# First batch's q norms partly from squares instead of a block product, and the late outputs stored in two halves

**Chip, cores, metric.** One core of one Trainium2 chip. The time is device microseconds of one execution; the profile's span, from the first to the last instruction, is about 1.8 us shorter. Times in the text are us from the start of the span unless they are called execution times.

## The reference, cut to what matters

```python
# B, N, C = 4, 6144, 256;  tau = 1
qn = q / (norm(q, axis=1) + 1e-6);  kn = k / (norm(k, axis=1) + 1e-6)   # over N
s = kn.transpose(0, 2, 1) @ qn / tau            # per batch a 256 x 256 matrix
a = softmax(s, -1);  x = v @ a                  # 24576 x 256
h = max(x @ w1, x @ w2, x @ w3);  out = h @ w_out        # d_ff = 768
```

Only the 256 x 256 softmax of the **first** batch stands alone at the head of the kernel. Those of the others are computed beside the big products.

## The kernel before

The kernel folds `a` into the weights (`aw = a @ w`), so the bulk is `h = v @ aw` (line L360) and `out = h @ w_out` (L380). For batch 0 it loads k and q, takes the q-by-k product into two PSUM banks (`gram`), and the q-by-q product of each half beside it in the same bank; its diagonal holds the squared norms.

```python
        for tp in range(NG // 2):                       # 24 pairs of rows
            for j in range(CC):
                PE.matmul(ps[j][:, 0:C], lhsT=qt[:, tsl, jsl], rhs=kt[:, tsl, :], ...)          # L178
                PE.matmul(ps[j][:, C:C + P], lhsT=qt[:, tsl, jsl], rhs=qt[:, tsl, jsl], ...)    # L180
    # ... cut ...
    def softmax_t(ps, rkb):
        for j in range(CC):                             # masked sum = diagonal        # L253
            DVE.tensor_tensor_reduce(out=scr, in0=ps[j][:, C:C + P], in1=ident, ..., accum_out=n2q[:, j:j + 1])
        ACT.activation(out=lnq, in_=n2q, func=AF.Ln)
        ACT.activation(out=rq, in_=lnq, func=AF.Exp, scale=-0.5, bias=neg_ln_tau)
        return exp_t([ps[j][:, 0:C] for j in range(CC)], rkb, rq)
    # ... cut ...
    ps = gram(0)
    for i in range(6):                                  # fill TensorE's time           # L436
        PE.matmul(warm_ps, lhsT=ident, rhs=warm, ...)
    et = softmax_t(*ps)
    v_transpose_pe(0)
    rinv = aw_first(et, aw)                             # first products with et        # L306
    v_transpose(1)                                      # transposing transfer of v of chunk 1, on SyncE's queue
    hold_loads(1)                                       # GpSimd reads the transposed tile: waits until it has landed
    POOL.dma_start(out=wo_sb, in_=moe_w_out...)         # only then the load of w_out   # L450
    # ... cut ...
            if t == TPC - 1:
                SP.dma_start(out=out_r[gi // NCH, gi % NCH], in_=st["o"])               # L386
```

## Time and profile before

| | before |
|---|---|
| execution time, three runs | 575.91 to 576.07 us |
| TensorE busy | 555.2 of 574.1 us, 97% |
| warm-up weight loads start | 34.00 |
| first h product (L360) | 37.47 |
| first o product (L380), asks for w_out | 50.58 |
| last store issued, end of span | 570.72, 574.09 |

The first is in the timeline near 50 us (columns: start, duration, engine, line, operation):

```profile
45.05 0.19 POOL L447 COPY guard<-vt_sb 128x1 bf16<-128x1 bf16 x1 [7.99 <-DMA vt_sb<-v_sb]
45.28 0.83 POOL L450 DMA_DIRECT2D wo_sb<-in_moe_w_out_dram  x1
...
50.58 0.82 PE L380 MATMUL o_ps<-wo_sb,ht_sb 128*128 128x256 bf16 x6
```

The load of w_out is issued only when the transposed v of chunk 1 has landed. It takes 5.2 us from issue to landing (the profile's time to landing of this tile), so it is there at 50.5, and TensorE asks for it at 50.58. There is 0.1 us to spare.

The second is at the very end, in the waits of SyncE's queue (engine and line, what it waited for, us in total, times, longest):

```profile
SPq L533 <- DMA out_dram<-o_sb: 1.6, 3, 0.9
```

The program ends when SyncE has gone through a row of waits for its stores, and three of these waits find a store that is still under way.

### The profile page before, as it was taken

The page shows a single profiled execution, that of the slowest core. Times are in us where ns is not written, and L with a number is a line of the kernel's source. Part 1 is how long each engine was busy: PE and PEld are TensorE (multiplying, and loading weights), DVE is VectorE, ACT ScalarE, POOL GpSimd, SP SyncE. Part 2 cuts the span into 40 slices and gives each one's busy share as a digit, 9 for nine tenths or more (in the row PEclk, how much of TensorE's full clock was granted, in tenths as well). Part 3 has the DMA queues.
Part 4 walks back from the last instruction along what each step waited for, and adds up shares of the span by engine and source line. Part 5 has one row for each costly group of instructions (what it writes and reads, how often), then busy time and mean ns, then how long its engine had stood idle before and what let it go on. Part 6 is the DMA issues. An engine that isn't in the chain of part 4 may idle for free.

```text
span 574.1 us, 9430 instructions
## 1 busy us (share of the span) xinstructions
PE 555.2 (97%) x3361; PEld 331.9 (58%) x3362; DVE 407.6 (71%) x639; ACT 308.6 (54%) x537; POOL 227.3 (40%) x235
## 2 busy tenths in 40 slices
PE   3789999999999999999999999999999999999997
PEld 3665555555755555555575555555575555555565
DVE  0058777777577778777748777777848778778775
ACT  1044567677454466776735447767646444444443
POOL 4232357876721028776761007777760000000000
PEclk9999999999999999999999999999999999999999
DMA  9999998995598128887378526888535234322111
GB/s 143 107 145 153 137 181 124 156 136 122 89 124 160 56 79 149 129 157 121 75 130 134 117 69 102 157 133 136 121 83 124 66 83 129 74 92 75 56 73 75
DMA packets 76095, 65.63 MB, mean 114 GB/s; under 512 B 52368, under 2 KB 62224, under 8 KB 76048
## 3 DMA queue, kind: packets, MB, share of 16 engines
q0 software_dynamic: 18928, 26.48, 39.1%
q1 hardware_dynamic: 56976, 38.41, 23.5%
q8 instruction: 26, 0.43, 0.3%
q14 instruction: 21, 0.17, 0.1%
q10 hardware_dynamic: 144, 0.13, 0.1%
HBM read 78.64 MB, written 25.17 MB: 181 GB/s over the span
## 4 chain that ended last, share of the span: by engine, by line
PE 94%; DMA 5%; issue 0%; DVE 0%; POOL 0%; POOLq 0%
PE h_ps L360 65%; PE o_ps L380 21%; DMA q_sb<-in_q_dram 3%; PE gram L235 3%; PE ew_ps L282 2%; DMA k_sb<-in_k_dram 2%; PE o_ps L401 0%; PE gram L178 0%; PE ew_ps L306 0%; PE n_ps L216 0%; PE warm_ps L436 0%; PE n_ps L218 0%; PE gram L180 0%; POOL k_sb L99 0%; PE vt_ps L343 0%
## 5 line engine op out<-in xcount | busy, mean ns | idle before, releaser
L360 PE MATMUL h_ps<-vt_sb,aw_sb 128*128 128x512 bf16 (+1 forms) x1764 | 407.2, 375 | 0.1
L365 DVE TENSOR_TENSOR s_mx<-h_ps,s_mx 128x512 bf16<-128x512 f32 (+1 forms) x294 | 198.8, 676 | 97.6 <-ACT s_mx L364 96.5
L360 PEld LDWEIGHTS <-aw_sb 128*128 128x128 bf16 x1764 | 171.8, 98 | 161.0 <-DVE aw_sb L288 2.8
L364 ACT ACTIVATE s_mx<-h_ps 128x512 bf16<-128x512 f32 (+1 forms) x294 | 172.3, 586 | 131.4 <-PE h_ps L360 130.0
L366 DVE TENSOR_TENSOR ht_sb<-h_ps,s_mx 128x512 bf16<-128x512 f32 (+1 forms) x294 | 200.2, 681 | 31.4 <-PE o_ps L380 0.5
L204 POOL TENSOR_TENSOR acc<-acc,sq 128x768 f32<-128x768 f32 x90 | 147.6, 1650 | 70.7 <-ACT sq L198 70.5
L380 PE MATMUL o_ps<-wo_sb,ht_sb 128*128 128x256 bf16 x1128 | 153.9, 273 | 0.0
L380 PEld LDWEIGHTS <-ht_sb 128*128 128x128 bf16 x1128 | 110.4, 98 | 52.0
L383 ACT ACTIVATE o_sb<-o_ps 128x512 f32<-128x512 f32 x94 | 56.1, 597 | 82.6 <-PE o_ps L380 82.6
L110 POOL DMA_DIRECT2D v_sb<-in_v_dram x48 | 26.8, 562 | 89.0 <-DMA vt_sb<-v_sb 87.1
L198 ACT ACTIVATE sq<-q_sb 128x768 bf16<-128x768 fp8e4 x48 | 40.5, 845 | 0.0
L198 ACT ACTIVATE sq<-k_sb 128x768 bf16<-128x768 fp8e4 x48 | 40.1, 835 | 0.0
L201 POOL CAST acc<-sq 128x768 f32<-128x768 bf16 x6 | 4.9, 821 | 63.1 <-ACT sq L198 63.1
L102 POOL DMA_DIRECT2D q_sb<-in_q_dram x32 | 17.7, 552 | 10.7 <-DMA k_sb<-in_k_dram 9.7
L166 PE MATMUL kk<-k_sb 128*128 128x256 fp8e4 x48 | 7.8, 339 | 11.6 <-DVE k_sb L152 5.4
L235 PE MATMUL gram<-k_sb,q_sb 128*128 128x512 fp8e4 x144 | 16.8, 277 | 0.0
L99 POOL DMA_DIRECT2D k_sb<-in_k_dram x29 | 15.9, 551 | 1.0 <-POOLq L519 0.8
L235 PEld LDWEIGHTS <-q_sb 128*128 128x256 fp8e4 x144 | 15.9, 136 | 0.6
L285 ACT ACTIVATE aw_sb<-ew_ps,rinv 128x384 bf16<-128x384 f32 (+1 forms) x24 | 13.2, 555 | 5.7 <-PE ew_ps L282 4.8
L282 PE MATMUL ew_ps<-w_sb,et 128*128 128x384 bf16 (+1 forms) x96 | 15.6, 313 | 0.0
L178 PE MATMUL gram<-k_sb,q_sb 128*128 128x512 fp8e4 x48 | 10.8, 323 | 3.3 <-DMA q_sb<-in_q_dram 3.3
L166 PEld LDWEIGHTS <-k_sb 128*128 128x256 fp8e4 x48 | 6.5, 182 | 12.7 <-DMA k_sb<-in_k_dram 6.3
(60 smaller groups left out, 105.6 us busy)
## 6 DMA issues: line engine op xcount, KB each, us to landing
out_dram<-o_sb SPq DMA_DIRECT2D x47, 512.0 KB, 2.8
v_sb<-in_v_dram POOLq DMA_DIRECT2D x48, 256.0 KB, 3.9
k_sb<-in_k_dram POOLq DMA_DIRECT2D x24, 192.0 KB, 5.4
q_sb<-in_q_dram POOLq DMA_DIRECT2D x24, 192.0 KB, 6.7
k_sb<-in_k_dram POOLq DMA_DIRECT2D x5, 256.0 KB, 10.8
q_sb<-in_q_dram POOLq DMA_DIRECT2D x5, 256.0 KB, 19.4
w_sb<-in_moe_w_dram POOLq DMA_DIRECT2D x9, 128.0 KB, 5.7
kf<-in_k_dram SPq DMA_DIRECT2D x2, 512.0 KB, 4.3
```

What stands on the lines that cost most here:

```text
L102: POOL.dma_start(out=qk[b][0][:, g0:g0 + w, :], in_=q_r[b][:, g0:g0 + w, :])
L110: POOL.dma_start(out=t, in_=v_r[gi // NCH, gi % NCH])
L198: ACT.activation(out=sq, in_=src, func=AF.Square)
L204: POOL.tensor_tensor(out=acc, in0=acc, in1=sq, op=ALU.add)
L235: PE.matmul(g[:, j * C:(j + 1) * C], lhsT=qt[:, tsl, j * P:(j + 1) * P], rhs=kt[:, tsl, :], start=(tp == 0 and j == 0), stop=(tp == NG // ...
L282: PE.matmul(ew[:, :w], lhsT=et[:, j, ic * P:(ic + 1) * P], rhs=w_sb[m][:, j, fsl], start=(j == 0), stop=(j == CC - 1))
L360: PE.matmul(t.rearrange("p (t n) -> p t n", n=P), lhsT=aw[m][:, ic, fsl], rhs=vt[:, tsl, ic, :], start=(ic == 0), stop=(ic == CC - 1))
L364: ACT.activation(out=s_mx, in_=hp[0], func=AF.Copy)
L365: DVE.tensor_tensor(out=s_mx, in0=hp[1], in1=s_mx, op=ALU.max)
L366: DVE.tensor_tensor(out=ht, in0=hp[2], in1=s_mx, op=ALU.max)
L380: PE.matmul(st["ps"][:, half], lhsT=ht[:, fc, t * P:(t + 1) * P], rhs=wo_sb[:, fc, :], start=(fc == 0), stop=(fc == FC - 1))
L383: ACT.activation(out=st["o"][:, t - 1:t + 1, :].rearrange("p t d -> p (t d)"), in_=st["ps"], func=AF.Copy)
```

## The change

The aim: q norms must wait for the last q rows, then for TensorE, then for two masked sums on VectorE. The change takes the last four of a partition's 48 rows out of the q-by-q product and gets their part from squares (ScalarE and VectorE) summed by one-column products on TensorE. The other rows' diagonal is masked early and added to the same PSUM column. Besides, chunks 42 to 46 store their output in two halves. In the diff, tile allocations and some arguments are left out.

```diff
+            block = 2 * tp < NG - QT                        # QT = 4 rows: the pairs 22 and 23
+            if not block:
+                ACT.activation(out=sq[:, :, h0], in_=qt[:, tsl, h0], func=AF.Square)
+                DVE.tensor_tensor(out=sq[:, :, h1], in0=qt[:, tsl, h1], in1=qt[:, tsl, h1], op=ALU.mult)
             for j in range(CC):
                 PE.matmul(ps[j][:, 0:C], lhsT=qt[:, tsl, jsl], rhs=kt[:, tsl, :], ...)
-                PE.matmul(ps[j][:, C:C + P], lhsT=qt[:, tsl, jsl], rhs=qt[:, tsl, jsl], ...)
+                if block:
+                    PE.matmul(qq[:, jsl], lhsT=qt[:, tsl, jsl], rhs=qt[:, tsl, jsl], ...)
+            if 2 * tp == NG - QT - 2:                        # after pair 21
+                for j in range(CC):
+                    DVE.tensor_tensor(out=dqm[:, jsl], in0=qq[:, jsl], in1=ident, op=ALU.mult)
+            if not block:
+                for g in range(2):
+                    for j in range(CC):
+                        PE.matmul(nq[:, j:j + 1], lhsT=sq[:, g, j * P:(j + 1) * P], rhs=ones_c, ...)
+                if not last:
+                    for j in range(CC):                      # fp32
+                        PE.matmul(nq[:, j:j + 1], lhsT=dqm[:, j * P:(j + 1) * P], rhs=ones_f[:, 0:1], ...)
     # ... cut: Ln and Exp now read nq; softmax_t is gone ...
-                SP.dma_start(out=out_r[gi // NCH, gi % NCH], in_=st["o"])
+                parts = 2 if gi >= B * NCH - 6 else 1
+                for i in range(parts):
+                    SP.dma_start(out=out_r[..., i * w:(i + 1) * w, :], in_=st["o"][:, i * w:(i + 1) * w, :])
```

More of the change, by code (lines that the diff above doesn't have):

```diff
@@ L172, in gram @@
         ps = [xtile(f"gram{j}") for j in range(CC)]
+        qq = htile("qq")
+        nq = htile("nq")
+        QT = 4
         for tp in range(NG // 2):
@@ L175, in gram @@
             last = tp == NG // 2 - 1
+            block = 2 * tp < NG - QT
+            if not block:
+                sq = sm.tile([P, 2, C], BF16, name="sq_last")
+                h0, h1 = slice(0, P), slice(P, C)
+                ACT.activation(out=sq[:, :, h0], in_=qt[:, tsl, h0], func=AF.Square)
+                DVE.tensor_tensor(out=sq[:, :, h1], in0=qt[:, tsl, h1], in1=qt[:, tsl, h1], op=ALU.mult)
             for j in range(CC):
@@ L179, in gram @@
                           start=(tp == 0), stop=last, perf_mode=DR, skip_group_check=True)
-                PE.matmul(ps[j][:, C:C + P], lhsT=qt[:, tsl, jsl], rhs=qt[:, tsl, jsl],
-                          start=False, stop=last, perf_mode=DR, skip_group_check=True)
+                if block:
+                    PE.matmul(qq[:, jsl], lhsT=qt[:, tsl, jsl], rhs=qt[:, tsl, jsl], start=(tp == 0 and j == 0),
+                              stop=(2 * tp == NG - QT - 2), perf_mode=DR, skip_group_check=True)
+            if 2 * tp == NG - QT - 2:
+                dqm = sm.tile([P, C], FP32, name="dqm")
+                for j in range(CC):
+                    jsl = slice(j * P, (j + 1) * P)
+                    DVE.tensor_tensor(out=dqm[:, jsl], in0=qq[:, jsl], in1=ident, op=ALU.mult)
+            if not block:
+                for g in range(2):
+                    for j in range(CC):
+                        PE.matmul(nq[:, j:j + 1], lhsT=sq[:, g, j * P:(j + 1) * P], rhs=ones_c,
+                                  start=(2 * tp + g == NG - QT and j == 0), stop=(last and g == 1),
+                                  skip_group_check=True)
+                if not last:
+                    for j in range(CC):
+                        PE.matmul(nq[:, j:j + 1], lhsT=dqm[:, j * P:(j + 1) * P], rhs=ones_f[:, 0:1],
+                                  start=False, stop=False, skip_group_check=True)
             if tp == 11:
@@ L188, in gram @@
                 ACT.activation(out=rkb, in_=lnk, func=AF.Exp, scale=-0.5)
-        return ps, rkb
+        lnq = sm.tile([P, CC], FP32, name="lnq")
+        rq = sm.tile([P, CC], FP32, name="rq")
+        ACT.activation(out=lnq, in_=nq[:, 0:CC], func=AF.Ln)
+        ACT.activation(out=rq, in_=lnq, func=AF.Exp, scale=-0.5, bias=neg_ln_tau)
+        return [ps[j][:, 0:C] for j in range(CC)], rkb, rq
     SQW = 3
@@ L247, in exp_t @@
         return et
-    def softmax_t(ps, rkb):
-        n2q = sm.tile([P, CC], FP32, name="n2q")
-        scr = sm.tile([P, P], FP32, name="scr")
-        for j in range(CC):
-            DVE.tensor_tensor_reduce(out=scr, in0=ps[j][:, C:C + P], in1=ident, scale=1.0, scalar=0.0,
-                                     op0=ALU.mult, op1=ALU.add, accum_out=n2q[:, j:j + 1])
-        lnq = sm.tile([P, CC], FP32, name="lnq")
-        rq = sm.tile([P, CC], FP32, name="rq")
-        ACT.activation(out=lnq, in_=n2q, func=AF.Ln)
-        ACT.activation(out=rq, in_=lnq, func=AF.Exp, scale=-0.5, bias=neg_ln_tau)
-        return exp_t([ps[j][:, 0:C] for j in range(CC)], rkb, rq)
     def alloc_aw():
@@ L385, in step @@
             if t == TPC - 1:
-                SP.dma_start(out=out_r[gi // NCH, gi % NCH], in_=st["o"])
+                parts = 2 if gi >= B * NCH - 6 else 1
+                w = TPC // parts
+                for i in range(parts):
+                    SP.dma_start(out=out_r[gi // NCH, gi % NCH, :, i * w:(i + 1) * w, :],
+                                 in_=st["o"][:, i * w:(i + 1) * w, :])
                 del hts[gi]
@@ L430, in last_chunk @@
         SP.dma_start(out=dst[:, HT + 1, :], in_=o_sb[:, HT + 1, :])
-    ps = gram(0)
+    gs = gram(0)
     warm_ps = htile("warm_ps")
@@ L436 @@
         PE.matmul(warm_ps, lhsT=ident, rhs=warm, start=(i == 0), stop=(i == 5))
-    et = softmax_t(*ps)
+    et = exp_t(*gs)
     v_transpose_pe(0)
```

## The prediction

> **What bounds the kernel now.** I read the page's busy shares first, then the chain of work that ended last, then that chain and the timeline around the end of the first gram product, because the change works there.
>
> ```profile
> PE 555.2 (97%) x3361; PEld 331.9 (58%) x3362; DVE 407.6 (71%) x639; ACT 308.6 (54%) x537; POOL 227.3 (40%) x235
> ...
> PE 94%; DMA 5%; issue 0%; DVE 0%; POOL 0%; POOLq 0%
> ```
>
> TensorE (PE) is busy 97% of a 574.1 us span, and 94% of the chain is TensorE work. From about 38 us on it has no gap, so a microsecond lost or won before that point should move the whole rest. The question is therefore when TensorE gets through the head. This is its chain there (start, duration, what):
>
> ```profile
> 11.07 20.04 DMA q_sb<-in_q_dram
> 31.10 0.04 issue
> 31.15 0.32 PE gram L178
> ...
> 34.23 1.24 PE warm_ps L436 x5
> 35.47 0.45 PE vt_ps L343 x8
> 35.92 0.62 PE ew_ps L306 x4
> 36.53 0.08 PE rs_ps L300 x4
> 36.61 0.90 PE ew_ps L306 x8
> ```
>
> The reader is to see that after the q rows land at 31.1 the chain never leaves TensorE: rest of gram, six warm-up products, eight transposes of v, then the products with the softmax. The softmax itself is not on this chain. It runs beside it, as the timeline shows:
>
> ```profile
> 33.61 0.13 PEld L178 LDWEIGHTS <-q_sb 128*128 128x256 fp8e4 x1
> 34.00 0.98 PEld L436 LDWEIGHTS <-ident 128*128 128x128 bf16 x6
> 34.03 0.29 DVE L253 CUSTOM_DVE_ANT_0 scr<-gram,ident 128x128 f32<-128x128 f32 x1 [14.03 <-PE gram L180]
> ...
> 34.69 0.75 DVE L245 TENSOR_TENSOR e_in<-gram,rkb 128x256 f32<-128x256 f32 x2
> 34.81 0.20 ACT L257 ACTIVATE lnq<-n2q 128x2 f32<-128x2 f32 x1 [6.36 <-DVE n2q L253]
> 35.05 0.20 ACT L258 ACTIVATE rq<-lnq 128x2 f32<-128x2 f32 x1
> ...
> 35.28 0.91 ACT L246 ACTIVATE et<-e_in,rq 128x256 bf16<-128x256 f32 x2
> 35.31 0.61 PE L343 MATMUL vt_ps<-ident,v_sb 128*128 128x128 bf16 x8
> 35.84 0.41 PEld L306 LDWEIGHTS <-et 128*128 128x128 bf16 x4
> ```
>
> The first half of et is done at 35.28 + 0.91/2 = 35.74 us. TensorE ends its transposes and takes et at 35.84. The two paths meet within 0.1 us, so the six warm-up products just fill the softmax's time, and there is almost nothing to gain from a shorter softmax unless TensorE also gets to the warm-up sooner than 34.00.
>
> [...] every gram product runs in the order of the loop (row pairs 0.33 us apart, from 31.15 to 34.1), so a product that waits holds up all behind it. [...] The trace has an idle wait of 1.79 us before the weight load at 31.14, after which the product of the same form still took 0.28 us as before it, so a shorter stall costs no clock. [...] the masks of kk, two halves in one bank, start after the last product has ended at 18.14 + 1.26 = 19.40, not after the first half.
>
> ```profile
> 18.14 1.26 PE L166 MATMUL kk<-k_sb 128*128 128x256 fp8e4 x8 [1.20 <-DMA k_sb<-in_k_dram]
> 19.51 0.49 DVE L171 TENSOR_TENSOR dkm<-kk,ident 128x128 f32<-128x128 f32 x2 [14.15 <-PE kk L166]
> ```
>
> **The change part by part.** *Removed:* four q-by-q products in the last two row pairs (L180, 0.056 us each at their spacing of 0.06: 0.22 us of TensorE), and on VectorE two masked sums with their reads (0.29 + 0.08 each, from 34.03 to 34.77). *Added:* for each of the last two pairs a square on ScalarE and one on VectorE, four products of one column; once, two masks of qq on VectorE and two fp32 one-column products (two passes each).
>
> Everything goes by the emission order, which the kernel fixes on each engine. VectorE: masks of qq, square of pair 22, square of pair 23, e_in. TensorE: gram of pair 22, its norm products, the fp32 ones, gram of pair 23, its norm products, warm-up. So TensorE, which ran through at this place, now waits for VectorE in mid-gram.
>
> Step by step, in us from the start. Up to pair 21 nothing changes: its last q-by-q product starts at 33.15 and lasts 0.22, so qq is complete at 33.37. The masks follow 0.07 later, 33.44, and take 0.49 as the two of kk did: 33.93. [...] (The half on ScalarE is out of the way: 256 of the 768 elements that take 0.84 there, some 0.4 us, started when the rows landed near 33.0.) TensorE had finished the gram of pair 22 at 33.20 + 2 x 0.11 = 33.42 and idled 0.9. Norm products of pair 22: load and first pass 0.1, the others at the 0.064 at which rs_ps loads its weights, 34.55. The fp32 pair: the same form in later batches takes four passes, 0.34 on the chain,
>
> ```profile
> 158.60 0.43 PE n_ps L216 x2
> 159.03 0.34 PE n_ps L218 x4
> ```
>
> so 34.90. Gram of pair 23: 0.22 plus a weight load that nothing hides, 35.13. (Its rows landed at 33.6, and both squares were ready by about 34.6.) Its four norm products, 0.26: **35.4**. The warm-up begins there instead of at 34.0.
>
> The softmax gains back nothing. Ln starts 0.2 later (35.6), rq is ready by 36.05, the first half of et by 36.5; but TensorE is at the warm-up until 36.7 and at the transposes until 37.2, so et waits for TensorE. The warm-up, which was free filling, becomes 1.28 us of pure delay. From the first product with et on the order of events is as before, 1.4 us later: row sums, evictions, first chunk. The v tile (read at 35.1 before) and the weights come by transfers that don't wait for TensorE, so they are there even more surely. Two more tiles in the rotation of six PSUM buffers are released before their turn (qq at 33.9, nq when Ln has read it, near 35.8, its next writer being at 37.2 or later).
>
> *The late stores.* For five chunks (42 to 46), one store of 512 KB becomes two of 256 KB. Both are issued after the last eviction of the chunk, so none starts earlier. The added cost is one issue of 0.33 us on SyncE, which waits most of the time. The last of the five is issued near 563.1 and lands some 3 us later; the end hangs on the last chunk's own stores, issued at 570.57 and 570.72 with 2 us to landing. I count 0.0.
>
> Sum: 576.07 + 1.4 = 577.47; I take **577.4**, since some of the small latencies may be counted twice.
>
> **Rivals.** *A: the intended gain.* If TensorE didn't stall, rq would follow the landing of the last rows (33.6) by a square of 0.4, four products of 0.25 with 0.15 of drain, and Ln and Exp of 0.44: about 34.85 against 35.25, 0.4 us sooner, 575.7. For it: the long wait of ScalarE for n2q (6.36 us) is what the change shortens. Against it: even then TensorE would start its warm-up no sooner than 33.6 + 0.4 + 0.25 = 34.25, later than now, and the chain runs over TensorE. *B: the stall is smaller*, if the first mask starts as soon as its own half of qq is there (33.24) and the square takes 0.3: then 0.2 to 0.4 us less delay, 577.0. *C: the stall costs a clock step or collides further on*, for instance a wait for a PSUM buffer in the first aw products: 578 to 579. The 1.79 us wait that cost no clock speaks against it. *D: the split stores delay the transposes of v on the same queue.* TensorE has no gap in that stretch and the transposed tiles are two chunks ahead (some 20 us), so this would make 0.
>
> **Range and chances.** The three runs of before lie within 0.16 us, so noise plays no part. The delay is a sum of about eight small steps, each perhaps 0.1 off, and one that can go by another path (B): +0.5 to +2.0, which gives 576.6 to 578.1. Two per cent would be 11.5 us, far beyond any of the rivals: within 2% at 0.98, faster and slower 0.01 each.
>
> **What would show it.** Right: in the profile of the changed kernel the warm-up weight loads start near 35.4; there is a TensorE wait of about 0.9 us for VectorE's square before a norm product of pair 22; Ln no longer waits for VectorE but for the nq products; et is finished before TensorE asks for it; the first h product starts near 38.9 instead of 37.47; the last chunk's spacing and the two last landings are unchanged. Wrong: warm-up before 34.3, or a start of the first h product that moved by less than 0.5 us, would mean that the order on VectorE or TensorE is not the emitted one; a first h product moved by 1.4 with an unmoved end would mean slack later that I did not see; a change after 560 us only would point to the stores.

What the traces of this case do not show is cut from the prediction, and the cuts are marked. One cut holds a term of the sum: the time of VectorE's square of pair 22, which took the chain from 33.93 to about 34.26. With it the sum came to 35.4 for the start of the warm-up against 34.00, so +1.4 us and 577.47; the 0.9 us of idle time and the steps after it rest on that term. Measured afterwards, one such square takes 0.41 us (seventh experiment) and two in a row 0.75 (third). Of the small latencies, the 0.07 from qq to the masks was 0.04 (33.36 to 33.40, third experiment), and the 0.15 of drain in rival A is an estimate that can be held against 0.163 us, the time of one row-sum product (L300) in the profile before.

## More of the kernel before

TensorE is the bound from about 38 us on: with no gap after that, whatever delays its first h product delays the end. The prediction shows the lines for this. Two things that it did not look at decide part of the result, and the profile before holds both.

## The result, and the profile after

The execution time went from 576.06 us (median of 6 runs) to 577.65 us (median of 6). A ratio is the mean time of one kernel's fast runs over that of the other's of the same rounds, so it is not quite the ratio of the two medians: 1.0022, with a 95% interval from 1.0008 to 1.0037. That is 0.2% slower. Two of the six runs after and one before were slow (590 us and more), and the two medians take them in; of the fast runs alone, with a seventh run after (576.83), they are 576.04 and 577.50: +1.46 us.

**Which runs are compared.** Among the fast runs there is a further step: those with a mean granted TensorE clock of 0.996 or 0.997 take 577.5 to 577.9 us for the kernel before (one 581.88), against 575.7 to 576.1 with a clock of 0.999 or 1.0. Below I quote the median of the fast runs whose clock is 0.998 or above, beside the same figure for the kernel before on the same chip. It also leaves out two more runs that count as fast (579.82 of the first experiment, clock 0.994, and 582.72 of the twelfth, 0.997).

The profile recorded with the result fell into the slow state, so the changed kernel was run again (the first experiment); that profile is fast, execution time 577.43 us. Its busy shares first:

```profile
PE 555.6 (97%) x3370; PEld 331.8 (58%) x3370; DVE 408.1 (71%) x639; ACT 309.2 (54%) x539; POOL 227.1 (39%) x235
```

TensorE's busy time grew by 0.4 us only, while the span grew by 1.55 us, so most of the loss is waits. Then the timeline of the head:

```profile
33.66 0.49 DVE L197 TENSOR_TENSOR dqm<-qq,ident 128x128 f32<-128x128 f32 x2 [13.63 <-PE qq L191]
33.94 0.42 ACT L184 ACTIVATE sq_last<-q_sb 128x256 bf16<-128x256 fp8e4 x1 [0.31 <-DMA q_sb<-in_q_dram]
34.06 0.75 DVE L185 TENSOR_TENSOR sq_last<-q_sb 128x256 bf16<-128x256 fp8e4 x2
34.53 0.14 PEld L201 LDWEIGHTS <-sq_last 128*128 128x128 bf16 x3 [0.75 <-DVE sq_last L185]
34.60 0.52 PEld L206 LDWEIGHTS nq<-ones_f,dqm 128*128 128x128 f32 x4
34.96 0.30 PEld L188 LDWEIGHTS <-q_sb 128*128 128x256 fp8e4 x2
35.32 0.17 PEld L201 LDWEIGHTS <-sq_last 128*128 128x128 bf16 x4
35.42 0.98 PEld L458 LDWEIGHTS <-ident 128*128 128x128 bf16 x6
35.62 0.17 ACT L217 ACTIVATE lnq<-nq 128x2 f32<-128x2 f32 x1 [1.25 <-PE nq L201]
36.05 0.91 ACT L276 ACTIVATE et<-e_in,rq 128x256 bf16<-128x256 f32 x2
37.12 0.37 PEld L324 LDWEIGHTS <-et 128*128 128x128 bf16 x4
38.85 1.04 PE L378 MATMUL h_ps<-vt_sb,aw_sb 128*128 128x512 bf16 x4
```

The reader is to see the stall in the fourth line: TensorE waits 0.75 us for VectorE's square, which stands in VectorE's queue behind the two masks. The gram of the last pair (sixth line), whose rows were in at 33.9, comes only at 34.96. The warm-up loads start at 35.42 against 34.00. And et, begun at 36.05, has its first half at 36.5, while TensorE takes it at 37.12: it was ready too soon by 0.6, where before it was ready just in time. In this execution the last q rows landed 0.3 us later than in the profile before (33.94 against 33.6). Of the runs with the same head, the third experiment has them at 33.58, and there the warm-up starts at 35.15 and the first h product at 38.60: **1.15 and 1.13 us late**. Its lines:

```profile
33.40 0.49 DVE L197 TENSOR_TENSOR dqm<-qq,ident 128x128 f32<-128x128 f32 x2 [13.54 <-PE qq L191]
34.27 0.14 PEld L201 LDWEIGHTS <-sq_last 128*128 128x128 bf16 x3 [0.76 <-DVE sq_last L185]
35.15 0.98 PEld L454 LDWEIGHTS <-ident 128*128 128x128 bf16 x6
...
38.60 1.25 PE L378 MATMUL h_ps<-vt_sb,aw_sb 128*128 128x512 bf16 x5
```

Then the loads of chunk 1, in the same timeline further on:

```profile
47.03 0.18 POOL L469 COPY guard<-vt_sb 128x1 bf16<-128x1 bf16 x1 [9.62 <-DMA vt_sb<-v_sb]
47.26 0.83 POOL L472 DMA_DIRECT2D wo_sb<-in_moe_w_out_dram  x1
...
52.46 0.70 PE L398 MATMUL o_ps<-wo_sb,ht_sb 128*128 128x256 bf16 x5 [0.32 <-DMA wo_sb<-in_moe_w_out_dram]
```

The load of w_out starts at 47.26 instead of 45.28, since the transposed v that holds it back took longer to land. By tile, of the kernel before and of the changed one:

```profile
DMA to landing us min/median/max: 2.9/2.9/2.9
```

```profile
DMA to landing us min/median/max: 4.5/4.5/4.5
```

So w_out lands at about 52.5, and now TensorE has to wait for it. How much this costs: from the first h product to the first o product the kernel before takes 50.58 - 37.47 = 13.11 us without a wait. 38.85 + 13.11 = 51.96, so the start at 52.46 is 0.50 late. (The profile's 0.32 counts from the modelled end of the product before, which overlaps.)

Last, the end: the last store is issued at 572.57 (1.85 later than before), but the span ends at 575.64, only 1.55 later.

```profile
SPq L555 <- DMA out_dram<-o_sb: 1.0, 2, 0.6
```

Here 0.30 us came back, after the last store was issued. For this profile the account closes: 0.25 (the head as a whole later than in the third experiment, the first h product at 38.85 against 38.60) + 1.13 (head) + 0.50 (w_out) - 0.30 (end) = 1.58 against 1.55 by the spans.

### The profile page after: what moved, and what is told of

It is laid out like the page before. It is cut to its first block, busy times and chain, and to the rows that moved or that the text cites. A ratio compares the mean times of both kernels' runs of the same rounds, so it can differ in the third digit from the quotient of the medians.

```text
span 597.5 us, 9464 instructions
## 1 busy us (share of the span) xinstructions
PE 562.8 (94%) x3369; PEld 333.9 (56%) x3370; DVE 409.1 (68%) x639; ACT 309.6 (52%) x539; POOL 226.9 (38%) x235
## 4 chain that ended last, share of the span: by engine, by line
PE 80%; DMA 18%; POOL 1%; issue 0%; ACT 0%; DVE 0%; POOLq 0%; ACTq 0%
PE h_ps L378 56%; PE o_ps L398 19%; DMA vt_sb<-v_sb 6%; DMA k_sb<-in_k_dram 4%; DMA v_sb<-in_v_dram 3%; DMA q_sb<-in_q_dram 3%; PE gram L265 3%; PE ew_ps L300 2%; DMA wo_sb<-in_moe_w_out_dram 1%; POOL k_sb L99 0%; PE o_ps L423 0%; POOL acc L234 0%; POOL w_sb L136 0%; PE n_ps L246 0%; PE n_ps L248 0%
## 5 line engine op out<-in xcount | busy, mean ns | idle before, releaser
L378 PE MATMUL h_ps<-vt_sb,aw_sb 128*128 128x512 bf16 (+1 forms) x1764 | 413.6, 378 | 15.1 <-DMA vt_sb<-v_sb 14.6
L300 PE MATMUL ew_ps<-w_sb,et 128*128 128x384 bf16 (+1 forms) x96 | 15.6, 313 | 0.0
```

Source lines behind the costliest of these rows:

```text
L300: PE.matmul(ew[:, :w], lhsT=et[:, j, ic * P:(ic + 1) * P], rhs=w_sb[m][:, j, fsl], start=(j == 0), stop=(j == CC - 1))
L378: PE.matmul(t.rearrange("p (t n) -> p t n", n=P), lhsT=aw[m][:, ic, fsl], rhs=vt[:, tsl, ic, :], start=(ic == 0), stop=(ic == CC - 1))
```

## The experiments

Theory: the loss is the stall of TensorE in mid-gram for VectorE, passed on through a warm-up that fills nothing any more. Rivals: the softmax chain or the clock sets the head; the loss or a gain is at the stores; a load in the first chunk takes part. Execution times are medians as said above, "before" being on the same chip.

| run | us | before | difference |
|---|---|---|---|
| changed kernel again | 577.13 | 575.87 | +1.26 |
| split stores only | 575.57 | 575.87 | -0.30 |
| new norms only | 577.51 | 575.87 | +1.64 |
| changed, 1 warm-up product | 576.04 | 575.87 | +0.17 |
| before, 1 warm-up product | 575.82 | 575.85 | -0.03 |
| square of pair 22 on ScalarE | 577.00 | 575.85 | +1.15 |
| reordered norms | 577.18 | 575.85 | +1.33 |
| reordered, 2 warm-up products | 577.10 (one run) | 575.85 | +1.25 |
| first five stores split | 575.47 | 575.95 | -0.48 |
| last eight stores split | 576.02 | 575.95 | +0.07 |
| split stores, w_out early | 575.57 | 575.95 | -0.38 |
| reordered, 2 warm-up, w_out early | 575.57 | 575.95 | -0.38 |

The intervals of the ratios, which take in all fast runs, are 0.13% to 0.5% to either side, so single differences of 0.3 us are below them; those I rely on are supported by the profiles too. All kernels gave correct results.

**1. The changed kernel again** (no edit).

> The changed kernel unaltered, because its profile on record fell into the slow state. Stall theory: in a fast profile the warm-up weight loads start at 35.2 us (as in the slow profile) against 34.0 before, the first h product near 38.6 against 37.47, no gap of TensorE afterwards; time +1.2 to +1.6 us over the kernel before. Rival (the loss comes later, in the first chunk or at the stores): the fast profile shows a head 1.2 us later but a further gap of TensorE after 39 us.

The head came as the stall theory says, and the rival of a further gap is right as well: the wait for w_out. The loss has two places, not one.

**2. The split stores alone**, in the kernel before.

```diff
-                SP.dma_start(out=out_r[gi // NCH, gi % NCH], in_=st["o"])
+                (two stores where gi >= B * NCH - 6, as in the change)
```

> The kernel before with only the late stores split in two. Stall theory: no effect, 576.0, within 0.2 us of the kernel before, since the end hangs on the last chunk's own stores. Rival (the stores cost or save time at the end): 0.5 us or more either way.

I expected nothing; it gained 0.30 us (575.48 to 575.88 in six runs). From the issue of the last store to the end it took 573.82 - 570.68 = 3.14 us against 3.37. So the stores do something, after the last of them.

**3. The new norms alone**, the changed kernel with single stores.

> The changed kernel with the single late stores of the kernel before. Stall theory: the whole loss is here, the same time as the changed kernel, 576.8 to 577.7. Rival (stores): back to 576.0, or a different loss than the full change.

577.51 us, 0.4 more than the whole change, which is the stores' gain again within the noise. Its profile gives the loss without mixing: first h product 38.60 (+1.13), first o product 52.49 where 38.60 + 13.11 = 51.71 (+0.78 for w_out), end 575.99 against 574.09: +1.90 = 1.13 + 0.78 within 0.01. The profiled run took 577.77, 0.26 above the median of this kernel, so w_out cost less than 0.78 in most of its runs.

**4. One warm-up product in the changed kernel.**

```diff
-    for i in range(6):
+    for i in range(1):
```

> The changed kernel with one warm-up product in place of six. Stall theory: after the stall et is ready (36.3 us) before TensorE is through warm-up and transposes (36.9), so five products of 0.21 us are delay; TensorE would reach et at 35.19 + 0.21 + 0.53 = 35.9 and wait until about 36.35: 0.5 to 0.6 us faster than the changed kernel, still 0.5 or more slower than the kernel before. Rival (the softmax chain, not TensorE, sets the first product with et): no gain. Rival (clock): without the warm-up products the clock drops and the time grows by 1 us or more.

It gained 1.1 us, nearly twice what I expected. The stall theory's part is in the head:

```profile
35.91 0.91 ACT L276 ACTIVATE et<-e_in,rq 128x256 bf16<-128x256 f32 x2
...
36.47 0.33 PEld L324 LDWEIGHTS <-et 128*128 128x128 bf16 x4 [0.22 <-ACT et L276]
```

Now TensorE waits for et. The first h product starts 4.30 us after the last rows landed (38.01 - 33.71), against 5.02 in the third experiment: 0.7 less. The other part is that w_out was in time here (the transposed v took 3.2 us), so the wait of 0.5 fell away too. No sign of a lower clock: it was 1.0 in the profiled run, and 0.999 or 1.0 in all five.

**5. One warm-up product in the kernel before** (the same edit).

> The kernel before with one warm-up product in place of six. Theory that the warm-up only filled the softmax's time there: v is in and the first bank free at 35.1, et's first half ready at 35.74, so TensorE takes et at about 35.8 instead of 35.84: 0.0 to 0.1 us faster, that is 576.0. Rival (warm-up is delay here too): 0.5 us or more faster. Rival (it keeps the clock): slower by 1 us or more.

No gain: 575.82 against 575.85 (two runs with a clock of 0.998 and 0.999; the profile fell in the slow state, though its head looks like that of before, with the first h product at 37.42). The five products taken away cost nothing before and 0.7 us after the change. Taken with the fourth experiment this shows that the warm-up turned from filling into delay.

**6. The whole square of pair 22 on ScalarE.**

```diff
-                DVE.tensor_tensor(out=sq[:, :, h1], in0=qt[:, tsl, h1], in1=qt[:, tsl, h1], op=ALU.mult)
+                if last:
+                    DVE.tensor_tensor(...)
+                else:
+                    ACT.activation(out=sq[:, :, h1], in_=qt[:, tsl, h1], func=AF.Square)
```

> The changed kernel with both halves of the square of pair 22 on ScalarE, so VectorE does only the masks before the fp32 products. Stall theory: norm products of pair 22 run at about 33.7, TensorE waits only for the masks (33.92), fp32 products until 34.3, gram of pair 23 and its norms until 34.9, so the warm-up starts 0.3 us sooner than 35.19 and the time is 0.3 us below the changed kernel. Rival (the added TensorE work, not the wait, is the loss): no change.

The head moved more than expected: warm-up at 34.50 and first h product at 37.94, 0.65 earlier than in the third experiment. So having the square of pair 22 in VectorE's queue cost 0.65 us of the late warm-up: TensorE's wait for it was real delay, as the theory has it. The other 0.50 (34.50 against 34.00) is left to the added products and the wait for the masks, which this run doesn't separate; in the third experiment the loads of the fp32 pair alone hold the place from 34.34 to 34.70. But the time hardly moved (577.00), because of this line of TensorE's waits:

```profile
PE o_ps L401 <- DMA wo_sb<-in_moe_w_out_dram: 0.7, 1, 0.7
```

**7. and 8. The norm products after the gram of the last pair**, the masked diagonal in bf16, and the whole square of pair 22 on ScalarE as in the sixth, with six and with two warm-up products.

```diff
-            (norm products and fp32 products of pair 22 before the gram of pair 23)
+            if last:      # squares of pair 22, then dqm (now bf16), then squares of pair 23
+                for n, col in enumerate(cols):
+                    for j in range(CC):
+                        PE.matmul(nq[:, j:j + 1], lhsT=col[:, j * P:(j + 1) * P], rhs=ones_c, ...)
```

> The changed kernel with the gram of pair 23 ahead of all norm products, both halves of the square of pair 22 on ScalarE, and the masked diagonal in bf16 (one pass per product); six warm-up products. Stall theory: norm products from 34.0 to 34.5, warm-up from 34.5 instead of 35.19: 0.6 to 0.7 us faster than the changed kernel, still 0.4 to 0.5 slower than the kernel before, since the warm-up starts 0.5 later than 34.00 there. Rival: if waits don't matter, as the changed kernel.

> As the reordered kernel, with two warm-up products in place of six. Here the intended shorter softmax can show: norms done by 34.5, rq by 35.1, et's first half by 35.6, TensorE at the transposes from 35.1 (v lands) to 35.65. Stall theory: 0.1 to 0.3 us faster than the kernel before, 575.8. Rival (a landing of the first weights bounds it): equal to the kernel before, 576.0.

Both heads came earlier than expected (warm-up at 34.20 in both; first h product at 37.64 and 37.32, the latter earlier than the 37.47 of before), and neither time moved. The whole gain went into the wait for w_out, here of the eighth:

```profile
PE o_ps L400 <- DMA wo_sb<-in_moe_w_out_dram: 1.5, 1, 1.5
PE ew_ps L326 <- DMA w_sb<-in_moe_w_dram: 0.2, 1, 0.2
```

Put side by side, the start of the first o product shows where the head stopped mattering ("asks" is the first h product + 13.11):

| kernel | first h | asks for w_out | first o | late by | transposed v, to landing |
|---|---|---|---|---|---|
| before | 37.47 | 50.58 | 50.58 | 0 | 2.9 |
| changed, again | 38.85 | 51.96 | 52.46 | 0.50 | 4.5 |
| new norms only | 38.60 | 51.71 | 52.49 | 0.78 | 4.9 |
| changed, 1 warm-up | 38.01 | 51.12 | 51.13 | 0 | 3.2 |
| square on ScalarE | 37.94 | 51.05 | 51.95 | 0.90 | 4.3 |
| reordered | 37.64 | 50.75 | 52.20 | 1.45 | 4.9 |
| reordered, 2 warm-up | 37.32 | 50.43 | 52.13 | 1.70 | 4.8 |

Where the transposed v takes 4.3 us or more, w_out comes at 51.9 to 52.5 whatever the head does. The account holds for each of these kernels: the shift of the first h product against 37.47, plus the lateness, less 0.30 where the stores are split, gives +1.58, +1.91, +0.24, +1.07, +1.32 and +1.25 us in the order of the table from its second row, and the profiled runs took +1.56, +1.90, +0.27, +1.14, +1.33 and +1.25 more than the kernel before on their chip.

**9. and 10. Which stores are split.** The transfers of these queues use eight completion semaphores in turn, and at the end SyncE waits for the eight in a fixed order, some 0.06 to 0.07 us each even when nothing is awaited. Before the change the last store falls on the third of the eight (the fourth wait in all), so five waits remain after its landing. Five more stores move it by five places, to the eighth. The transposes of v take their turns among the same eight. The ninth splits five stores that are far from the end, the tenth splits eight, a full turn.

```diff
-                parts = 2 if gi >= B * NCH - 6 else 1
+                parts = 2 if gi < 5 else 1                # ninth
+                parts = 2 if gi >= B * NCH - 9 else 1     # tenth
```

> The kernel before with the stores of the first five chunks split in two, those of the late ones whole. Rotation theory: the eight semaphores of the stores are taken in turn, five more stores move the last store from the fourth of the waits at the end to the last one, so only about 0.07 us of waits come after its landing in place of 0.37: from the last store's issue to the end 3.1 us in place of 3.4, 0.3 us faster, though no late store is touched. Rival (smaller late transfers help the end): no gain here.

> The kernel before with the stores of the last eight whole chunks split in two. Rotation theory: eight more stores leave the rotation where it was, the last store again has the fourth of the waits: 3.4 us from the last issue to the end, no gain. Rival (smaller late transfers): the gain of the five split stores or more, 0.3 us or above.

The rotation theory held in both: 575.47 us, in all five runs below the lowest of the kernel before on that chip, with no late store touched, and 576.02 us, no gain, with eight late stores split. The ends of the traces (not a view of the profile, but read from the same trace):

```
            last store's semaphore full   row of waits done   span ends
before            572.86                      573.24          574.09
last eight        573.18                      573.56          574.40
first five        572.76                      572.85          573.67
```

0.38 us of waits after the landing in the first two, 0.09 in the third. In the tenth the store itself landed 0.2 later after its issue than in the others (2.36 against 2.14), which I don't explain.

**11. and 12. The load of w_out ahead of the hold**, in the kernel of the second experiment and in that of the eighth.

```diff
-    hold_loads(1)
     POOL.dma_start(out=wo_sb, in_=moe_w_out.rearrange("(fc p) d -> p fc d", p=P))
+    hold_loads(1)
```

> The kernel before with the split late stores and the load of w_out issued before, not after, the wait for the transposed v of chunk 1. Theory of the two levels (576.0 and 577.6 in fast executions of the kernel before): the upper level is the first o product waiting for w_out when that transpose lands after 4.3 to 4.9 us in place of 2.9. Then the upper level is gone: all fast executions near 575.6. Rival (the levels have another cause): some executions near 577.2. Danger: w_out and the transpose share the transfer engines and the transpose lands later; it has until 47.9 us.

> The reordered kernel with two warm-up products, split stores, and w_out loaded early. There the first h product started at 37.32 against 37.47 before, but a wait of 1.5 us for w_out took it back. Theory: without that wait the shorter softmax shows at last: 575.5, about 0.15 below the kernel before with the split stores, 0.4 to 0.6 below the kernel before. Rival (something else in the first chunk takes it back): 576 or more.

The twelfth confirms the second place of the loss: the transposed v took 5.0 us to land there and no wait for w_out is left:

```profile
50.53 0.82 PE L400 MATMUL o_ps<-wo_sb,ht_sb 128*128 128x256 bf16 x6
```

The first o product starts at the first h product, 37.42, plus 13.11, and the time falls from 577.10 (+1.25 against the kernel before on that chip) to 575.57 (-0.38). But the shorter softmax still shows nothing beyond the split stores (575.57 both). In the head TensorE now waits 0.2 us for a set of first weights, as in the eighth experiment. That rival fits, though no run brings these weights in earlier; the first h product of the kernel before, at 37.47, is within 0.15 us of those with that wait (37.32 and 37.42).

The danger named for the eleventh did not come: between 41 and 47.5 us its profile has the loads' queue q0 and the transpose's q1 on the same 16 engines, for 47.7% and 20.7% of their time, and the transposed v landed in 3.1 us, against 2.9 before. The eleventh missed in one point. I took the level at 577.5 us of the kernel before for executions in which w_out was late. With w_out early one run of six still took 577.42, at a clock of 0.997. All eight runs of the kernel before at that level (577.48 to 577.94) have a clock of 0.996 or 0.997, so the level goes with a lower mean clock there. It doesn't in every kernel: the eighth's two runs at 0.997 and 0.996 took 576.77 and 577.15, against 577.10 for its run at 0.999. What sets the lower clock off is open; no profile fell in it with the kernel before. After TensorE's first product its longest idle time in the profile before, at a clock of 1.0, is 1.6 us (before 31.14).

The lowest measured is the kernel before with five more stores (575.47 us with the first five split, 0.08% under it). The interval of its ratio, 0.9975 to 1.0001, still takes in no change; what supports a gain of about 0.3 is the table of ends above, and part of the 0.48 may be noise.

## Why the prediction was right or wrong

The time (577.65 by all runs, 577.50 by the fast ones, 577.13 by those of full clock in the second round, against 577.4 predicted) lies in the range. The larger part of the mechanism, the stall and the warm-up that passes it on, was the one predicted; a wait that the prediction ruled out (w_out) and a gain that it put at nothing (the end) came in besides. That the sum lies so near is partly luck: its errors cancel.

- **VectorE's order, TensorE's wait: right.** The masks start at 33.40 in the third experiment (predicted 33.44), that is after both halves of qq, so rival B is out. Both engines keep to the emitted order: VectorE starts the squares at 33.80, behind the masks, though the rows of pair 22 were in at 32.85, and TensorE the gram of pair 23 at 34.70, though its rows were in at 33.58. The norm products of pair 22 resume at 34.27 (predicted after the square at 34.26), the stall is 0.76 by the profile (predicted 0.9 of idle time), and taking VectorE's square away (sixth experiment) takes 0.65 us off the head.
- **The step from there to the warm-up: mis-sized by 0.26.** Predicted 34.26 to 35.4 = 1.14; measured 34.27 to 35.15 = 0.88. The term is that of the norm products, which I counted at 0.064 each from the row sums. One of pair 22 ran before the stall (33.42); the three after it take 0.07 where 0.29 was predicted, and the four of the last pair 0.09 (35.06 to 35.15) where 0.26 was, the last three of these starting 0.025 to 0.026 apart once the first had started. The gram of pair 23 between them took more than predicted, 0.36 (34.70 to 35.06) against 0.23.
- **The warm-up becomes pure delay: right**, by the fourth and fifth experiments (0.7 us in the changed kernel, nothing before).
- **"The v tile and the weights come by transfers that don't wait for TensorE, so they are there even more surely": this step failed.** It holds for v of chunk 0 and for the first weights, but not for w_out. Its chain doesn't wait for TensorE either (the transposing transfer is issued at 42.13 before, at 42.11 in the third experiment): the load of w_out is issued when the transposed v of chunk 1 has landed, and that took 4.5 to 4.9 us with the new norms where it had taken 2.9. So w_out had 0.1 us to spare before, and was 0.5 to 0.8 late after, although TensorE asked for it over 1.1 us later. The prediction looked for waits on the path up to the first h product and called everything after it free of gaps, without asking how nearly a load met its use. Rival C ("collides further on, a wait for a PSUM buffer") had the right shape and the wrong object.
- **The late stores, "I count 0.0": wrong by 0.3.** The reason given (the end hangs on the last chunk's own stores) fits the traces. What was missed is what follows the last landing, and that the number of stores moves it.

Head 1.13 + w_out 0.5 to 0.8 - stores 0.3 = 1.3 to 1.6 by the profiles of the first and third experiments and the stores, against +1.26 and +1.46 measured; +1.4 was predicted for the head alone.

Open: why the transposed v of chunk 1 lands later with the new norms. In seven of the eight profiles with them it took 4.3 to 5.0 us, in the fourth experiment's 3.2; in the six profiles with the old norms 2.8 to 3.1. Over all 47 transposing transfers the median is 3.7 or more against 3.4 in the kernel before. It isn't when TensorE gets through the head, since the reordered kernels have the head of before within 0.2 us. The change also adds and removes small tiles ahead of the v tiles in memory, so their addresses may differ; whether that matters I did not try.

The packed traces hold a clue (packets by queue, not a view of the profile). In each of the 14 profiles one 16 KB packet of queue q8, which the page lists as "instruction", falls near this transpose, whose 1056 packets are on q1. In the seven profiles with the late transpose, the q8 packet starts, at 42.99 to 44.75, while 109 to 1056 packets of the transpose have not ended, and the last of them ends at 45.8 to 46.4. In the other seven, the fourth experiment's among them, it starts, at 44.53 to 45.32, with at most 8 left, and the last ends at 44.3 to 45.4. So the lateness goes with a packet of the instruction queue that falls into the transpose. No run moves that packet, so it is not shown as the cause, and it says nothing on the general shift from 3.4 to 3.7.

## What to carry to other kernels

Before taking a wait out of a head that TensorE already fills, look where each engine's own order puts the new instructions: a short job queued behind another on VectorE made TensorE stand still for 0.75 us in the middle of a product that needed nothing from it. When the first part moves, check every load that is first used soon after, with how much it has to spare; here a load with 0.1 us of slack turned late while TensorE asked for it later, and in the seventh and eighth experiments it took back the whole gain of a better order. And at the end of a program, what comes after the last transfer's landing is part of the time (here 0.38 or 0.09 us of waits): count it before putting a gain of a few tenths down to the size of the transfers.
